# Where the ring splits of a sequence's second half stand, and how many weight-rounding steps follow each product

## The chip, the cores and the metric

The kernel runs on one core of one Trainium2 chip, in one launch. The metric is the device time of that core in microseconds; each run is one execution, and the figure quoted for a kernel is the median of its runs. The profile comes from one further execution.

## What is computed

For 4 sequences of 768 tokens and 384 features, three layers follow each other. Cut to what matters here:

```python
x = delta_rule_attention(q, k, v, beta)          # 8 heads of 48, 768 steps
h = gelu_tanh(x @ w_in)                          # 384 -> 1024
u, v = h[..., :512], h[..., 512:]
v_n = (v - mean(v)) / sqrt(var(v) + 1e-6) * g_ln
v_s = einsum('ts,bsd->btd', w_sg, v_n) + b_sg    # mixing along the 768 tokens
x = x + (u * v_s) @ w_out                        # gates, then the projection
xk, xr = shifted_mix(x, mu_k), shifted_mix(x, mu_r)
out = sigmoid(xr @ w_r) * (relu(xk @ w_k) ** 2 @ w_v)
```

All products are made to float32 precision: each operand is split into a high and a low part (fp32r), and three TensorE products (high by high, high by low, low by high) are summed.

## The kernel before, in words

**Three stages.** The first (to about 340 us of the profile) runs the attention scan together with `x @ w_in`; it writes the normed `v` of each 128-token chunk to DRAM (`vn_d`) and `u` to `u_d`. The second (about 311 to 491 us) is the mixing stage, which the change touches. The third computes the last layer and is not changed.

**The mixing stage.** A sequence `b` has six token chunks `c` and two halves `t` of 384 output tokens each. `mix(b, t, d)` (L1067) makes one mixing product for 128 of the 512 features: 18 matmuls over the six chunks (`mix_mm`, L974), left operand the split chunk (`g` in the profile, "the ring"), right operand the split `w_sg` half (`sw0h`, `sw0l` for t = 0, `ws1h`, `ws1l` for t = 1). Its gates follow: on DVE `w` = product times `g_ln` plus `b_sg` (L1077), times `u` (L1079); on ACT the high part `gh` (L1080); on DVE the low part `gl` (L1083), which is issued one product later. `project(b, t)` (L1091) makes the half's projection: three products of 12 matmuls each (L151), each added into `xT` by DVE (L1099). On TensorE the order per sequence is: `begin`, which makes chunks 0 to 3 of all four products of t = 0 (48 matmuls, L984); the projection of the sequence before, half 1; the rest of the four t = 0 products; the t = 1 products d = 0, 1, 2; the projection of half 0; the t = 1 product d = 3. In the last sequence the projection of half 0 comes behind d = 3.

**The ring.** It has nine slots. A chunk of the next sequence is loaded from `vn_d` into a staging tile `st` by SP (L246) and split by `to_ring` (L907): ACT copies the high part (L120), and the low part is a subtraction, by DVE for chunks 0 and 3, by POOL for the others (L123). Chunks 0 to 2 are split behind `mix(b, 1, 1)` (`VD`), chunks 3 to 5 behind the last gates, those of `mix(b, 1, 3)`. The slots of chunks 3 to 5 are those which the current sequence's chunks 0 to 2 leave, so a split also waits until `mix(b, 1, 3)` has been read from them. "Boundary 0-1" below is the passage from sequence 0 to 1, and so on.

**The rounding jobs.** The weights `w_k`, `w_r` and `w_v` come as pairs of 32-bit words and are rounded beside the mixing stage (`narrow`, L154): a load into `raw`, an ACT copy (L164), four DVE steps (L169, L171, L173, L175), an integer addition by POOL (L177), the high part by ACT (L181), the low part by POOL (L182), a store to DRAM (L203). Blocks are 256 or 384 columns wide. `side(n)` (L1032) issues up to n DVE steps of jobs that are ready, with the other engines' instructions of a job as they come up; it is called behind each mixing product (`SD[0]` = 1) and behind each of the three products of a projection (`SD[1]` = 5). `turns` counts these places; a job's operation that is to be spaced comes one turn later in any case:

```python
            elif isinstance(c, tuple) and c[0]:
                e[0], e[2] = turns[0] + 1, c[1]
```

**What sets the order.** Every engine runs its instructions in the order in which this code issues them; in the mixing stage the order of PE, ACT, DVE, POOL and SP is as written, and no scheduler moves them. The last stage's inputs (`xm_hi`, L120) use memory that the jobs' `raw` buffers give back, so the first of them waits for the last store.

Of the kernel before, what the change touches and what calls it, by code (L numbers as in the profile page):

```python
# [40 lines left out]
EVERY = 12  # L41
NMIX = 12
LATE = 100
PUT = 2
BUDGET = 1.62
SLOT = 5.315
GSTEP = 3
# [14 lines left out]
NRAW = 3  # L62
NNA = 3
PD = 2
SD = (1, 5)
CS = (5, 4)
VF = (0, 3)
VD = 1
# [18 lines left out]
def fused_kernel(  # L87
# [66 lines left out]
    def narrow(dram, i, j, hi, lo, cw=CW, pool=stg, parts=None):  # L154

        w = CW if pool is stg else cw
        raw = pool.tile([P, 2 * w], U32, name="raw", bufs=NRAW)
        nc.sync.dma_start(out=raw[:, :2 * cw], in_=dram[i * P:(i + 1) * P, j:j + cw].bitcast(U32))  # L160
        w_lo = vw(raw, 0, [(2, cw)])
        w_hi = vw(raw, 1, [(2, cw)])
        yield 0
        yield 0, lambda: A.activation(w_lo.bitcast(I32), w_lo, AF.Copy, scale=2.0 ** -29)  # L164
        a = pool.tile([P, w], U32, name="na", bufs=NNA if pool is stg else 2)[:, :cw]
        af = a.bitcast(F32)
        t1 = cw / 1920 + 0.16
        t2 = cw / 960 + 0.16
        V.tensor_scalar(a, w_hi, 0x7FFFFFFF, None, op0=ALU.bitwise_and)  # L169
        yield t1  # L170
        V.tensor_scalar(af, af, E_LO_F, E_HI_F, op0=ALU.max, op1=ALU.min)  # L171
        yield t1
        V.tensor_scalar(a, a, 3, 0x3FFFFFFF, op0=ALU.logical_shift_left, op1=ALU.bitwise_and)  # L173
        yield t1
        V.scalar_tensor_tensor(a, w_hi, 0xC0000000, a, op0=ALU.bitwise_and, op1=ALU.bitwise_or)  # L175
        yield t2
        yield hops[0], lambda: G.tensor_tensor(a.bitcast(I32), a.bitcast(I32), w_lo.bitcast(I32), op=ALU.add)  # L177
        if hi is None:
            hi, lo = (raw[:, e * cw:e * cw + cw].bitcast(F32R) for e in range(2))
            parts.append(raw[:, :2 * cw].bitcast(F32).rearrange("p (x n) -> p x n", x=2))  # L180
        yield 1 + hops[0], lambda: A.activation(hi, af, AF.Copy)  # L181
        yield hops[0], lambda: G.tensor_tensor(lo, af, hi.bitcast(F32), op=ALU.subtract)  # L182

    def resident(dram, pool, name, nblk, n, j0=0, j1=None):
# [9 lines left out]
    def scratch(dram, name, nblk, n, cw=CW, pool=stg):  # L194

        d = dp.tile([nblk, P, 2, n], F32, name=name + "_d")

        def job(i, j):
            parts = []
            yield from narrow(dram, i, j, None, None, cw, pool, parts=parts)  # L200

            def put():
                nc.sync.dma_start(out=d[i, :, :, j:j + cw], in_=parts[0])  # L203

            yield PUT, put

        return d[:, :, 0], d[:, :, 1], [lambda i=i, j=j: job(i, j) for i in range(nblk) for j in range(0, n, cw)]

# [16 lines left out]
    hops = [1]  # L225
# [806 lines left out]
    def side(n):  # L1032

        while n > 0:
# [12 lines left out]
            c = next(e[1], None)  # L1047
            if c is None:
                live.remove(e)
                e[3].append(turns[0] + 1)  # L1050
            elif isinstance(c, tuple) and c[0]:
                e[0], e[2] = turns[0] + 1, c[1]
            elif isinstance(c, tuple):
                c[1]()
            else:
# [11 lines left out]
    def mix(b, t, d):  # L1067
# [3 lines left out]
            pt = ps.tile([P, HF], F32, name="ms")  # L1071
        for c in range(c0, 6):
            mix_mm(pt, b, t, d, c)
        if d == 0:
            gs[b, t] = [mp.tile([P, 4, DM], F32R, name=x) for x in ("gh", "gl")]
        w = vr.tile([P, DM], F32, name="w", bufs=2)
# [8 lines left out]
        if t == 1 and d == 3:  # L1085
            side(1)
            owing.pop()()
        side(SD[0])
        turns[0] += 1

    def project(b, t):  # L1091
        gh, gl = gs.pop((b, t))
        for f in range(3):
# [3 lines left out]
                             for c in range(4)])  # L1097
            xs = xT[:, b, f, 1 + t * DM:1 + t * DM + DM]
            V.tensor_tensor(xs, xs, pt[:, :DM], op=ALU.add)  # L1099
            side(SD[1])  # L1100
            turns[0] += 1

    load_u(0, 0)
# [1 line left out]
    for k, (b, t) in enumerate(halves):  # L1105
# [7 lines left out]
        for d in range(4):  # L1113
# [6 lines left out]
            if t == 1 and b + 1 < B:  # L1120
                if d == VD:
                    for c in range(3):
                        load_v(b + 1, c)
                    for c in range(3, 6):
                        fetch_v(b + 1, c)
                if d == 3:
                    for c in range(3, 6):
                        load_v(b + 1, c)
        while k == 7 and (live or lanes[1][0]):
            side(999)  # L1130
            turns[0] += 1
# [144 lines left out]
```

## Time and profile before

| | us |
|---|---|
| median of 3 runs | 739.75 |
| lowest and highest run | 736.57, 740.77 |
| the profiled execution's own time | 733.87 |
| its span, first to last instruction | 732.2 |
| TensorE busy in it | 679.5 (93%) |
| VectorE busy in it | 504.9 (69%) |

The profiled execution's time is 1.7 us over its span and 5.88 us under the median of the runs. The busy shares are means over all three stages; the mixing stage is read by itself, from the timeline of each engine. Times within the profile are us from the start of the span; a start of one instruction behind another on the same engine tells how late a queue is.

### The profile page before, as it was taken

The page shows a single profiled execution, that of the slowest core. Times are in us where ns is not written, and L with a number is a line of the kernel's source. Part 1 is how long each engine was busy: PE and PEld are TensorE (multiplying, and loading weights), DVE is VectorE, ACT ScalarE, POOL GpSimd, SP SyncE. Part 2 cuts the span into 40 slices and gives each one's busy share as a digit, 9 for nine tenths or more (in the row PEclk, how much of TensorE's full clock was granted, in tenths as well). Part 3 has the DMA queues.
Part 4 walks back from the last instruction along what each step waited for, and adds up shares of the span by engine and source line. Part 5 has one row for each costly group of instructions (what it writes and reads, how often), then busy time and mean ns, then how long its engine had stood idle before and what let it go on. Part 6 is the DMA issues. An engine that isn't in the chain of part 4 may idle for free.

```text
span 732.2 us, 24481 instructions
## 1 busy us (share of the span) xinstructions
PE 679.5 (93%) x10669; PEld 616.3 (84%) x10669; DVE 504.9 (69%) x992; ACT 366.7 (50%) x696; POOL 201.6 (28%) x257
## 2 busy tenths in 40 slices
PE   2567899999989999999999798999999999999998
PEld 2536678888879888899999698998989898999997
DVE  6999999876968965215969697879555564636251
ACT  2237576766757768734323233248354453625140
POOL 3133554443434553231353546340000000000000
PEclk9989999999999999999999999999999999999999
DMA  8503454455565557278645655539000000000000
GB/s 251 105 30 97 130 156 131 116 170 152 161 174 139 162 156 206 63 191 269 244 159 198 220 179 191 188 110 231 33 11 31 14 21 22 23 23 11 33 12 32
DMA packets 80938, 88.71 MB, mean 121 GB/s; under 512 B 24704, under 2 KB 63616, under 8 KB 80832
## 3 DMA queue, kind: packets, MB, share of 16 engines
q1 hardware_dynamic: 75520, 77.33, 35.2%
q0 software_dynamic: 5312, 9.83, 5.2%
q8 instruction: 83, 1.36, 0.8%
q14 instruction: 23, 0.19, 0.1%
HBM read 56.60 MB, written 25.82 MB: 113 GB/s over the span
## 4 chain that ended last, share of the span: by engine, by line
PE 76%; DVE 11%; issue 5%; DMA 4%; POOL 2%; ACT 1%; SPq 0%; POOLq 0%; ACTq 0%; DVEq 0%
PE ms L151 35%; PE ms L705 8%; PE ms L653 7%; PE ms L979 6%; PE ms L581 4%; PE rk L539 3%; PE sps L567 3%; PE rk L552 3%; PE rk L516 2%; PE ms L336 2%; PE ms L474 2%; DVE sg L358 1%; PE qk L519 1%; PE ms L744 1%; DVE w L1077 1%
## 5 line engine op out<-in xcount | busy, mean ns | idle before, releaser
L151 PE MATMUL ms<-wvh,sl 128*128 128x384 f32 x192 | 64.7, 337 | 0.0
L151 PE MATMUL ms<-wvl,sh 128*128 128x384 f32 x192 | 64.6, 337 | 0.0
L151 PE MATMUL ms<-wvh,sh 128*128 128x384 f32 x192 | 64.6, 336 | 0.0
L979 PE MATMUL ms<-sw0h,g 128*128 128x384 f32 x192 | 53.2, 350 | 7.6 <-ACT g L120 6.8
L177 POOL TENSOR_TENSOR na<-na,raw 128x256 int32<-128x256 int32 (+2 forms) x43 | 35.5, 826 | 89.4 <-DVE na L175 35.5
L151 PE MATMUL ms<-xm_hi,sw0h 128*128 128x512 f32 x144 | 56.3, 391 | 0.4 <-ACT xm_hi L120 0.4
L151 PE MATMUL ms<-xm_lo,sw0h 128*128 128x512 f32 x144 | 56.2, 390 | 0.2 <-DVE xm_lo L123 0.2
L151 PE MATMUL ms<-xm_hi,sw0l 128*128 128x512 f32 x144 | 56.1, 390 | 0.0
L123 DVE TENSOR_TENSOR sl<-sg,sh 128x512 fp32r<-128x512 f32 x48 | 33.0, 691 | 25.2 <-ACT sh L120 25.1
L979 PE MATMUL ms<-ws1h,g 128*128 128x384 f32 x192 | 49.9, 335 | 0.0
L1212 DVE TENSOR_TENSOR sg<-sg,ms 128x384 f32<-128x384 f32 x24 | 13.3, 553 | 50.8 <-PE ms L151 50.8
L358 DVE TENSOR_TENSOR sg<-sg,Yt 128x512 f32<-128x512 f32 (+4 forms) x72 | 43.5, 616 | 1.5
L120 ACT ACTIVATE sh<-sg 128x512 fp32r<-128x512 f32 x48 | 30.1, 631 | 28.2 <-DVE sg L1195 28.2
L979 PEld LDWEIGHTS ms<-sw0h,g 128*128 128x128 f32 x192 | 36.5, 197 | 9.1 <-ACT g L120 7.4
L1194 ACT ACTIVATE sg<-ms 128x512 f32<-128x512 f32 x48 | 28.6, 598 | 27.1 <-PE ms L151 24.1
L1080 ACT ACTIVATE gh<-w 128x384 fp32r<-128x384 f32 x32 | 16.8, 525 | 50.0 <-DVE w L1079 50.0
L1195 DVE TENSOR_TENSOR sg<-sg 128x512 f32<-128x512 f32 x48 | 33.1, 693 | 11.0 <-ACT sg L1194 10.8
L336 PEld LDWEIGHTS ms<-kT 64*32 64x32 f32 x640 | 19.5, 129 | 23.9 <-issue 17.0
L532 POOL TENSOR_SCALAR_AFFINE_SELECT SQ<-SQ 64x512 f32<-64x512 f32 x36 | 26.1, 724 | 48.9 <-ACT SQ L531 47.7
L181 ACT ACTIVATE raw<-na 128x256 fp32r<-128x256 f32 (+2 forms) x31 | 13.5, 436 | 51.3 <-POOL na L177 51.2
L345 ACT ACTIVATE sg<-ms 128x256 f32<-128x256 f32 x32 | 17.6, 578 | 41.2 <-PE ms L338 41.1
L338 PE MATMUL ms<-kT 64*32 64x64 f32 (+1 forms) x640 | 22.4, 232 | 16.4 <-issue 16.4
(244 smaller groups left out, 2203.1 us busy)
## 6 DMA issues: line engine op xcount, KB each, us to landing
u_d<-ug SPq DMA_DIRECT2D x24, 256.0 KB, 4.3
u<-u_d SPq DMA_DIRECT2D x16, 384.0 KB, 5.6
vn_d<-v SPq DMA_DIRECT2D x22, 256.0 KB, 2.8
vk<-in_vk_dram SPq DMA_DIRECT2D x24, 192.0 KB, 4.0
vk<-in_vk_dram SPq DMA_DIRECT2D x12, 384.0 KB, 4.8
st<-vn_d SPq DMA_DIRECT2D x18, 256.0 KB, 3.6
out_dram<-sg SPq DMA_DIRECT2D x24, 192.0 KB, 1.9
kT<-in_kt_d_dram SPq DMA_DIRECT2D x8, 512.0 KB, 4.6
```

Of the source, the lines that this page charges most:

```text
L120: A.activation(hi, src, AF.Copy)
L123: eng_lo.tensor_tensor(lo, src, hi.bitcast(F32), op=ALU.subtract)
L151: T.matmul(pt, lhsT=a, rhs=b, start=(i == 0), stop=(i == n - 1))
L177: yield hops[0], lambda: G.tensor_tensor(a.bitcast(I32), a.bitcast(I32), w_lo.bitcast(I32), op=ALU.add)
L336: T.matmul(gps[r:r + 32, p, c0:c1], lhsT=t[r:r + 64, u, 0:32], rhs=t[r:r + 64, u, c0:c1], start=True, stop=True)
L358: V.tensor_tensor(tv, vw(a_t, a_off, a_dims), vw(b_t, b_off, b_dims), op=ALU.mult)
L581: T.matmul(yps[b0:b0 + 64, (0, 1, 2, 6, 3, 4, 5, 7)[p], :], lhsT=cur[h][:, p, 0:64], rhs=cur[h][:, p, D:], start=True, stop=True)
L653: T.matmul(vstat[g, b], lhsT=a[:, c], rhs=w[:, c], start=first, stop=last)
L705: T.matmul(vstat["u"][:, 2 * P * d:2 * P * d + 2 * P], lhsT=w[:, c, ds_], rhs=a[:, c].rearrange("p b t -> p (b t)"), start=first, stop=last)
L979: T.matmul(pt[:, :DM], lhsT=v[:, ds_], rhs=w, start=(c == 0 and i == 0), stop=(c == 5 and i == 2))
L1194: A.activation(r, pt, AF.Relu)
L1195: V.tensor_tensor(r, r, r, op=ALU.mult)
```

## The change

Five edits, all of which act in the mixing stage alone (in the first stage `hops` is 1, and every operation has the spacing that it had):

1. `load_v` for chunks 3 to 5 is called inside `mix(b, 1, 3)`, behind its matmuls and ahead of its gates, and no more behind them.
2. Behind a mixing product `side` may issue 1 step in half 0 and 2 in half 1 (before: 1). Behind each product of a projection it may issue 6 for the projection of a half 1 and 3 for that of a half 0 (before: 5).
3. A job's spaced operations keep the spacing that they ask for. That of the high part is written as 2 turns (it was one turn in effect), that of the store as 1 (as in effect before).
4. A finished job's lane may start its next job in the same turn, not one later.
5. Constants: `SD` and `PUT` go, `SDM` and `SDP` come; `SDH` is used nowhere.

```diff
-PUT = 2
...
-SD = (1, 5)
+SDM = (1, 2)
+SDP = (6, 3)
+SDH = 2
...
-        yield 1 + hops[0], lambda: A.activation(hi, af, AF.Copy)
+        yield 2, lambda: A.activation(hi, af, AF.Copy)
...
-            yield PUT, put
+            yield 1 + hops[0], put
...
-                e[3].append(turns[0] + 1)
+                e[3].append(turns[0])
             elif isinstance(c, tuple) and c[0]:
-                e[0], e[2] = turns[0] + 1, c[1]
+                e[0], e[2] = turns[0] + c[0], c[1]
...
         for c in range(c0, 6):
             mix_mm(pt, b, t, d, c)
+        if t == 1 and d == 3 and b + 1 < B:
+            for c in range(3, 6):
+                load_v(b + 1, c)
...
-        side(SD[0])
+        side(SDM[t])
...
-            side(SD[1])
+            side(SDP[1 - t])
...
-                if d == 3:
-                    for c in range(3, 6):
-                        load_v(b + 1, c)
```

**DVE at boundary 1-2**, from the second addition of the projection of sequence 1, half 0, on. `g_7404` before and `g_7373` in the change are the same tile, chunk 3 of sequence 2. Lines of the changed kernel stand 1 to 4 higher (L1099 is L1103, L1077 is L1081, L1083 is L1087, L123 is L124). Before:

```order
L1099 TENSOR_TENSOR xT<-xT,ms 128x384
L171 TENSOR_SCALAR na<-na 128x384
L173 TENSOR_SCALAR na<-na 128x384
L175 SCALAR_TENSOR_TENSOR na<-raw,na 128x384
L1077 SCALAR_TENSOR_TENSOR w<-ms,g_sb,b_sb 128x384
L1079 TENSOR_TENSOR w<-w,u 128x384
L1083 TENSOR_TENSOR gl<-w,gh 128x384 x2
L123 TENSOR_TENSOR g_7404<-st_7264,g_7404 128x512
```

And in the change:

```order
L1103 TENSOR_TENSOR xT<-xT,ms 128x384
L172 TENSOR_SCALAR na<-na 128x384
L174 TENSOR_SCALAR na<-na 128x384
L176 SCALAR_TENSOR_TENSOR na<-raw,na 128x384
L1103 TENSOR_TENSOR xT<-xT,ms 128x384
L124 TENSOR_TENSOR g_7373<-st_7245,g_7373 128x512
L1081 SCALAR_TENSOR_TENSOR w<-ms,g_sb,b_sb 128x384
L1083 TENSOR_TENSOR w<-w,u 128x384
L1087 TENSOR_TENSOR gl<-w,gh 128x384
L170 TENSOR_SCALAR na<-raw 128x256
L1087 TENSOR_TENSOR gl<-w,gh 128x384
```

The split has passed the two gates and both low parts, and stands directly behind the last addition. Counted over the whole of sequence 1, from the first addition of the projection of sequence 0, half 1, up to the first gate of `mix(1, 1, 3)` before and up to the split in the change, DVE's queue holds 34 rounding steps before and 26 in the change. The same count for sequence 2 is 32 before and 35 in the change.

**ACT at the same place.** In the change:

```order
L165 ACTIVATE raw<-raw 128x384
L182 ACTIVATE raw<-na 128x256 x2
L121 ACTIVATE g_7373<-st_7245 128x512
L121 ACTIVATE g_7376<-st_7247 128x512
L121 ACTIVATE g_7379<-st_7249 128x512
L1084 ACTIVATE gh<-w 128x384
```

The three high parts of the ring stand ahead of the last `gh` and behind two high parts of rounding jobs; before, they stood behind that `gh` and one more high part.

**DVE behind the projection of sequence 1, half 1**, the first of its three products. In the change:

```order
L1103 TENSOR_TENSOR xT<-xT,ms 128x384
L176 SCALAR_TENSOR_TENSOR na<-raw,na 128x256
L170 TENSOR_SCALAR na<-raw 128x384
L172 TENSOR_SCALAR na<-na 128x384
L174 TENSOR_SCALAR na<-na 128x384
L176 SCALAR_TENSOR_TENSOR na<-raw,na 128x384
L170 TENSOR_SCALAR na<-raw 128x384
L1103 TENSOR_TENSOR xT<-xT,ms 128x384
```

Six steps lie between two additions where four lay before. Behind the second addition there are six against four, behind the third five against four. From the first addition to the low part of `mix(2, 0, 3)` it is 20 steps against 16.

## Rows read from the trace of the kernel before

**Rows 1.** The page's first part: busy us (share of span) xinstructions, engines by line.

```profile
PE 679.5 (93%) x10669; PEld 616.3 (84%) x10669; DVE 504.9 (69%) x992; ACT 366.7 (50%) x696; POOL 201.6 (28%) x257
```

**Rows 2.** Waits of PE, 310 to 510 us: waited for, total us, times, longest.

```profile
PE ms L979 <- ACT g L120: 6.8, 2, 4.8
PE ms L979 <- DVE g L123: 0.8, 2, 0.5
```

**Rows 3.** Busy time by stretch: us, PE, PEld, DVE, ACT, POOL, PEclk, DMA, GB/s.

```profile
358.49:369.96 11.47, 11.47 (x67) 11.47 (x67) 7.33 (x15) 4.03 (x9) 5.68 (x6) 1.00 0.73 236
396.23:414.68 18.45, 13.37 (x67) 12.53 (x67) 14.63 (x24) 5.80 (x13) 12.63 (x12) 0.91 0.63 202
440.93:455.45 14.52, 12.02 (x67) 11.38 (x67) 11.80 (x21) 5.21 (x11) 9.94 (x10) 1.00 0.60 208
410.40:414.60 4.20, 3.74 (x12) 3.23 (x13) 1.07 (x1) 1.49 (x4) 3.56 (x3) 0.59 0.98 304
```

**Rows 4.** PE's timeline, boundaries 1-2 and 2-3: start us, us, instruction, [idle before <-releaser].

```profile
405.44 0.34 PE L979 MATMUL ms<-sw0h,g 128*128 128x384 f32 x1
410.57 0.51 PE L979 MATMUL ms<-sw0h,g 128*128 128x384 f32 x1 [4.80 <-ACT g L120]
...
434.57 0.34 PE L151 MATMUL ms<-gh,wo_hi 128*128 128x384 f32 x1
...
450.14 0.34 PE L979 MATMUL ms<-sw0h,g 128*128 128x384 f32 x1
452.49 0.44 PE L979 MATMUL ms<-sw0h,g 128*128 128x384 f32 x1 [2.01 <-ACT g L120]
```

**Rows 5.** DVE's timeline, sequences 1 and 2.

```profile
372.28 0.56 DVE L1099 TENSOR_TENSOR xT<-xT,ms 128x384 f32<-128x384 f32 x1 [5.73 <-PE ms L151]
...
402.33 0.35 DVE L171 TENSOR_SCALAR na<-na 128x384 f32<-128x384 f32 x1
...
404.74 0.73 DVE L171 TENSOR_SCALAR na<-na 128x384 f32<-128x384 f32 x1
...
407.46 0.60 DVE L1077 SCALAR_TENSOR_TENSOR w<-ms,g_sb,b_sb 128x384 f32<-128x384 f32 x1
...
410.55 1.07 DVE L123 TENSOR_TENSOR g<-st,g 128x512 fp32r<-128x512 f32 x1 [0.37 <-ACT g L120]
...
433.31 0.55 DVE L1083 TENSOR_TENSOR gl<-w,gh 128x384 fp32r<-128x384 f32 x1
...
448.17 1.25 DVE L175 SCALAR_TENSOR_TENSOR na<-raw,na 128x384 uint32<-128x384 uint32 x1
449.34 0.60 DVE L1077 SCALAR_TENSOR_TENSOR w<-ms,g_sb,b_sb 128x384 f32<-128x384 f32 x1
...
452.47 1.07 DVE L123 TENSOR_TENSOR g<-st,g 128x512 fp32r<-128x512 f32 x1 [0.38 <-ACT g L120]
```

**Rows 6.** ACT's timeline at boundary 1-2.

```profile
409.07 0.52 ACT L1080 ACTIVATE gh<-w 128x384 fp32r<-128x384 f32 x1 [3.26 <-DVE w L1079]
...
409.91 1.66 ACT L120 ACTIVATE g<-st 128x512 fp32r<-128x512 f32 x3
```

**Rows 7.** DVE busy in 372 to 450 us, lines L169, L171, L173, L175 in turn.

```profile
372.00:450.00 78.00, 7.35 (x16) 0.98 0.55 184
372.00:450.00 78.00, 8.05 (x16) 0.98 0.55 184
372.00:450.00 78.00, 7.84 (x17) 0.98 0.55 184
372.00:450.00 78.00, 9.79 (x17) 0.98 0.55 184
```

**Rows 8.** The chain that ended last, at the end of the stage: start us, us, what.

```profile
488.71 2.30 DMA wv_d<-raw
...
491.12 0.64 ACT xm_hi L120
```

**Rows 9.** Waits of ACT, 310 to 510 us.

```profile
ACT raw L181 <- POOL na L177: 49.3, 15, 9.4
```

## The prediction

> **What bounds the kernel now.** I read the page's busy times first: TensorE is busy for 93% of the span, VectorE for 69% [rows 1]. Those are means over three stages, so the next view is what TensorE waits for in the mixing stage. Two waits carry nearly all of it, both in front of a mixing product's matmul: 6.8 us, two times, until ACT has made a high part of the ring, and 0.8 us, two times, until DVE has made a low part [rows 2]. The timeline of TensorE puts them at two places: in front of chunk 3 of sequence 2, and of sequence 3 [rows 4].
>
> Their price is best read by comparing equal work. The last product of a sequence and `begin` of the next are 66 matmuls at each of the three boundaries. They took 11.47 us at boundary 0-1, 18.45 us at 1-2 and 14.52 us at 2-3 [rows 3]. The first shows no idle TensorE (11.47 us busy of 11.47), so the other two lose 6.98 and 3.05 us, 10.03 us together. Of the 6.98 us, 4.80 us are one wait [rows 4]; part of the rest is the clock: behind that wait the granted clock was 0.59 for 4.20 us, where 0.5 is the 1.2 GHz level and 1.00 the 2.4 GHz level [rows 3]. At 2-3 the idle time was shorter and the clock stayed at 1.00.
>
> Why is the ring late? Not for lack of a transfer or of a slot. ACT began the three high parts at 409.91 us, directly behind the last `gh` at 409.07 us [rows 6], and that `gh` had to wait for DVE's gates, which began at 407.46 us [rows 5]. TensorE had begun the last matmul in front of the wait at 405.44 us [rows 4]. So DVE is some 8 us behind TensorE there, and the ring waits in its queue. At the start of the sequence DVE was not late: at 372.28 us it stood idle for 5.73 us until TensorE gave it the first addition [rows 5]. The lateness grows within each sequence and ends there, at `begin`. That is the resource to follow: DVE's queue from this first addition to the split of chunk 3.
>
> **The change, part by part.**
>
> *The split ahead of the gates.* Two gates, two low parts and ACT's last `gh` no longer lie in front of it. DVE reaches the split where it reached the gates before: at 407.46 us less what the steps change, instead of 410.55 us; at boundary 2-3 at 449.34 us instead of 452.47 us [rows 5]. Everything behind the split moves back by its own 1.07 us or less. The gates' results are next used by the projection of half 1, which comes behind `begin`: hidden at 1-2 by the microseconds that the gates gain there, and about in time at 2-3.
>
> *The steps.* Rounding steps took 7.35, 8.05, 7.84 and 9.79 us for 16, 16, 17 and 17 of them [rows 7]: 33.03 us for 66, 0.50 us each. In sequence 1 the queue holds 26 in front of the split, not 34: 8 x 0.50 = 4.0 us earlier. The split of chunk 3 would begin at 407.46 - 4.0 = 403.5 us and end 1.07 us later, at 404.5 us. TensorE needs the high part one matmul behind 405.44 us, at about 405.6 us, and the low part two further on, at 406.0 us. So the wait goes, with 1.4 us to spare, the clock stays up, and the whole 6.98 us come back. In sequence 2 there are 35 for 32: 3 x 0.50 = 1.5 us later. The split begins at 449.34 + 1.5 = 450.8 us and ends at 451.9 us. By the row at 450.14 us TensorE needs the low part at 450.7 us [rows 4], so about 1.2 us of the 3.05 us stay.
>
> *Bounds of a step.* A 384-wide L171 took 0.35 us alone and 0.73 us beside POOL; the longest step in the rows took 1.25 us [rows 5]. At 0.35 us the 8 steps less are worth 2.8 us and the 3 more cost 1.1 us; at 1.25 us it is 10 us and 3.8 us. At the low price the split of 1-2 ends at 405.7 us, still in time, and 0.8 us of the wait at 2-3 stay; at the high price TensorE waits at 2-3 as long as before. I take the mean, since the steps moved are of all four lines.
>
> *More steps behind the projection of a half 1.* In front of the low part of `mix(2, 0, 3)` there are 20 steps for 16, which makes it 2.0 us later at 0.50 us. It ended at 433.31 + 0.55 = 433.9 us [rows 5], so then at 435.9 us. The projection of half 0 begins at 434.57 us [rows 4] and takes this low part with its 11th matmul, 1.8 us on, at 436.3 us. That is hidden, with 0.4 us to spare; at 1.25 us per step it would be 2.5 us late. A wait here would delay TensorE and so shorten the one at 2-3, and the two aren't added.
>
> *Spacing and lanes.* These change the order, not the number of instructions. The extra turn puts the high part of a job further behind POOL's addition; ACT waited for that addition 15 times, 49.3 us in all [rows 9], beside a TensorE that mostly did not wait. I cost it at nothing: ACT has the time, unless the ring's high parts stand behind such a wait (the third rival). SP's loads of the ring's chunks stay in their places among the stores.
>
> *The end of the stage.* The last store landed 2.30 us behind its issue at 488.71 us, and the last stage's first input followed at 491.12 us [rows 8], while TensorE finished its projections. The steps of the last job stand among the last gates in both orders, one place earlier in the change, so the chain should move with TensorE. I cost it at 0, between -0.4 us (the wait is gone) and +2 us.
>
> **Sum.** 6.98 + 3.05 - 1.2 = 8.8 us. The profiled execution took 733.87 us; less 8.8 us that is 725.1 us. It lies 5.9 us under the median of the runs, 739.75 us, and I carry the same difference over to that: 731.0 us. Runs of one kernel lie up to 3 us from their median, so about 0.5%, 3.7 us, is what a measurement of this kernel can tell from no change.
>
> **Rivals.**
>
> *Sequence 2 gives it back.* If its steps run mostly beside POOL's work, at the long price, boundary 2-3 keeps its 3.05 us and the projection of half 0 begins to wait, say 1 us. The row of 0.35 against 0.73 us speaks for it; the mean of 0.50 us, which already holds such steps, against. Then 6.98 - 1.0 = 6.0 us: 733.8 us. The Trainium skill, GPSIMD Engine Reference, section Specifications, says that GpSimd shares its SBUF interfaces with VectorE and contends with DVE instructions in a 2-port mode or with two SBUF inputs. By that rule, packing six steps behind a product whose POOL work runs beside them is no free move; the trace agrees on the stretching, by the two L171 rows.
>
> *The end does not move.* If the last rounding jobs keep their absolute times, the last store still lands at 491 us and TensorE, 9 us early, waits there. Against it: the steps are bound to the gates in DVE's order. For it: a job is longer by one turn, and stores share the transfer engines with the reload of `w_k`. With 7 of the 8.8 us lost it is 738 us.
>
> *The split stops the queue it was put in front of.* DVE can't pass it. ACT's high part of chunk 3 stands behind two high parts of rounding jobs, which wait for POOL; the longest such wait was 9.4 us [rows 9]. If ACT is held so long at both boundaries, DVE, which has no other work to go to, is held with it, the gates come later still, and TensorE waits for the ring some 9 us at each instead of 5.1 and 2.5 us: 10 us more, 750 us. It decides from the point where ACT reaches the split later than about 412 us. Against it: POOL's addition for these two jobs follows DVE steps that stand a projection product ahead of the split, about 3 us before. The Trainium skill, TensorE: Matmul & The Clock Gate, section on the array's architectural detail, states that the queues of ACT and DVE are strictly first in, first out; the trace agrees (high parts at 409.91 us only behind the `gh` at 409.07 us), and it is what makes this rival possible.
>
> *It does not act.* The budgets are upper limits; where no job is ready nothing is issued, and the order shows 0 steps behind one product of each kind. But the split's new place and the 26 for 34 are in the order, so this only trims the sum.
>
> **How the numbers follow.** Forecast 0.60 (both waits mostly gone, 729 to 734 us); sequence 2 gives it back 0.20 (733 to 736 us); the end does not move 0.11 (736 to 741 us); the split stops the queue 0.09 (745 us and more). Faster by over 0.5% is under 736.0 us: the first case, nearly all of the second, a little of the third: 0.79. Within 0.5%: 0.13. Slower: 0.08. The range reaches from 727.5 us (all of 10.0 us, and 2 us of scatter) to 737.5 us (the second case, and part of the third).
>
> **What would show it.** TensorE's 66 matmuls at boundary 1-2 take about 11.5 us with a clock of 1.00, and at 2-3 between 11.5 and 13 us. DVE's split of chunk 3 begins some 2 us ahead of TensorE's need at 1-2 and about with it at 2-3. No wait for `gl` at the projection of sequence 2. The first `xm_hi` comes about 9 us earlier. I am wrong if the span of the mixing stage shrinks and the time doesn't, if DVE stands idle in front of L124 for microseconds, or if a new wait of PE for `gl` is as long as the one removed.

## The result and the profile after

The changed kernel is slower: its median is 742.41 us against 736.41 us for the kernel before (17 runs each), a ratio of 1.0086 with a 95% interval of 1.0062 to 1.0111, or some 6 us. The forecast was 731.0 us, its range 727.5 to 737.5 us. (The ratios here and below are estimated from the single runs; the quotient of two medians differs from them by up to 0.2% and is 1.0081 here.) Its profiled execution has a span of 740.2 us, 8.0 us over the 732.2 us of before.

The 8.0 us are first put in their places. TensorE reached the mixing stage 2.8 us later (314.56 instead of 311.74 us). That is no effect of the change: the program of the first stage is the same, and over the profiles of all kernels of this study with that first stage the same moment lies anywhere from 309.23 to 317.25 us. The rest arose in the mixing stage. The first view is TensorE's waits from there on (what waited, for what: us in total, times, longest), after the change:

```profile
PE ms L980 <- ACT g L121: 5.4, 1, 5.4
PE ms L980 <- DVE g L124: 3.6, 1, 3.6
...
PE ms L152 <- DVE gl L1087: 0.7, 1, 0.7
```

These are the two kinds of wait of [rows 2], each one time instead of two, and in total longer: 9.0 us instead of 7.6. The busy times by stretch say where (columns as in [rows 3]); the stretches are boundary 1-2, the projection of half 0 in sequence 2, boundary 2-3, and two pieces of the last:

```profile
399.02:410.49 11.47, 11.47 (x67) 11.47 (x67) 9.45 (x15) 3.82 (x9) 8.61 (x8) 1.00 0.51 168
430.40:437.74 7.34, 6.62 (x38) 6.30 (x37) 5.24 (x13) 2.28 (x5) 0.74 (x1) 1.00 0.47 161
437.74:462.55 24.81, 15.78 (x68) 14.91 (x67) 15.89 (x25) 7.13 (x16) 11.13 (x10) 0.77 0.47 159
446.40:451.80 5.40, 5.33 (x18) 5.11 (x19) 5.28 (x8) 2.33 (x6) 3.57 (x3) 0.54 0.71 257
459.00:464.50 5.50, 5.32 (x17) 5.32 (x18) 3.87 (x7) 2.17 (x5) 3.64 (x4) 0.50 0.14 49
```

Boundary 1-2 is what the prediction said, to the hundredth: 11.47 us instead of 18.45, no idle TensorE, clock 1.00. But boundary 2-3 takes 24.81 us, 10.3 us more than the 14.52 us of before. Of its 13.34 us over 11.47, 9.03 us are idle time (24.81 less 15.78 us busy), and the other 4.31 us are matmuls at a lower clock: behind the two waits, of 5.45 and 3.58 us, the granted clock was 0.54 and 0.50, at or near the 1.2 GHz level. The projection in front of it is 0.98 us longer, the one behind it 1.09 us (clock again). So: 2.8 - 7.0 + 1.0 + 10.3 + 1.1 - 0.2 (the end of the stage) = 8.0 us.

The question is boundary 2-3. DVE's timeline there:

```profile
433.44 0.61 DVE L1081 SCALAR_TENSOR_TENSOR w<-ms,g_sb,b_sb 128x384 f32<-128x384 f32 x1
...
435.03 0.42 DVE L176 SCALAR_TENSOR_TENSOR na<-raw,na 128x256 uint32<-128x256 uint32 x1
437.35 0.30 DVE L170 TENSOR_SCALAR na<-raw 128x256 uint32<-128x256 uint32 x1 [1.91 <-DMA raw<-in_w_k_dram]
446.45 0.69 DVE L124 TENSOR_TENSOR g<-st,g 128x512 fp32r<-128x512 f32 x1 [8.80 <-ACT g L121]
447.06 0.61 DVE L1081 SCALAR_TENSOR_TENSOR w<-ms,g_sb,b_sb 128x384 f32<-128x384 f32 x1
```

From the gates of one product to those of the next DVE takes 13.6 us, of which it stands idle 1.91 us in front of a job's first step, whose raw words are not there, and 8.80 us in front of a split. This is not the split that the change moved: it is that of chunk 0, behind the product t = 1, d = 1, whose place the change leaves alone. The chain of waits (start us, us, what; pieces of under 0.1 us left out) says what was late:

```profile
434.94 3.05 DMA wk_d<-raw
438.04 0.33 SPq L161
438.42 3.55 DMA wv_d<-raw
442.02 0.33 SPq L161
442.40 3.37 DMA st<-vn_d
445.79 0.64 ACT g L121
```

And SP's timeline shows how the row of the chain began:

```profile
426.77 0.33 SPq L161 DMA_DIRECT2D raw<-in_w_k_dram  x1
427.14 0.43 SPq L204 DMA_DIRECT2D wv_d<-raw  x1
430.67 0.33 SPq L161 DMA_DIRECT2D raw<-in_w_v_dram  x1
431.10 0.56 SPq L204 DMA_DIRECT2D wk_d<-raw  x1
434.56 0.33 SPq L161 DMA_DIRECT2D raw<-in_w_k_dram  x1
...
442.02 0.33 SPq L161 DMA_DIRECT2D raw<-in_w_v_dram  x1
442.40 1.37 SPq L247 DMA_DIRECT2D st<-vn_d  x3
```

A store, then the load of the next job, which goes into a `raw` buffer that a store gives back, so that SP stands until that store has landed; then the next store. The five loads of raw words from 426.77 to 442.02 us follow each other at 3.5 to 4.0 us, each behind a store, and the loads of the ring's chunks 0 to 2 (L247) behind them: 442.40 us instead of 430.14 us before. The waits of SP from 426 to 442.3 us are 14.6 us of 16.3:

```profile
SPq L161 <- DMA wk_d<-raw: 8.4, 3, 3.0
SPq L161 <- DMA wv_d<-raw: 6.2, 2, 3.1
```

In the kernel before SP did the same, only less often. There the ring's loads stood behind these (SP's timeline of before):

```profile
421.06 0.33 SPq L160 DMA_DIRECT2D raw<-in_w_v_dram  x1
421.43 0.56 SPq L203 DMA_DIRECT2D wk_d<-raw  x1
424.92 0.33 SPq L160 DMA_DIRECT2D raw<-in_w_k_dram  x1
427.26 0.56 SPq L203 DMA_DIRECT2D wk_d<-raw  x1
429.76 0.33 SPq L160 DMA_DIRECT2D raw<-in_w_k_dram  x1
430.14 1.37 SPq L246 DMA_DIRECT2D st<-vn_d  x3
```

How much less often can be counted on SP's timeline, from the last of the ring's loads for sequence 2 to the first of those for sequence 3. Before, 8 loads of raw words and 8 stores stand there, and the loads waited 19.7 us for stores in a stretch of 40.2 us. In the change there are 11 and 11, and the loads waited 31.6 us in 53.5 us. So the longer waits for stores are 11.9 of the 13.3 us by which the stretch grew. The times 430.14 and 442.40 us differ by 12.3 us, of which 2.8 us are the later start of the stage: counted from TensorE's first matmul of the stage, the ring's loads go out 9.4 us later.

### The profile page after: what moved, and what is told of

It reads as the page before. It is cut to its first block, busy times and chain, and to the rows that moved or that the text cites. A ratio compares the mean times of both kernels' runs of the same rounds, so it can differ in the third digit from the quotient of the medians.

```text
span 740.2 us, 24476 instructions
## 1 busy us (share of the span) xinstructions
PE 685.4 (93%) x10669; PEld 621.4 (84%) x10669; DVE 507.6 (69%) x992; ACT 366.9 (50%) x696; POOL 204.2 (28%) x257
## 4 chain that ended last, share of the span: by engine, by line
PE 80%; DVE 10%; issue 4%; DMA 3%; POOL 1%; ACT 1%; SPq 0%; POOLq 0%; DVEq 0%; ACTq 0%
PE ms L152 36%; PE ms L980 9%; PE ms L706 8%; PE ms L654 7%; PE ms L582 4%; PE sps L568 3%; PE rk L540 3%; PE rk L553 3%; PE rk L517 2%; PE ms L337 2%; PE ms L475 2%; DVE sg L359 1%; PE qk L520 1%; PE ms L745 1%; DVE w L1083 1%
## 5 line engine op out<-in xcount | busy, mean ns | idle before, releaser
L178 POOL TENSOR_TENSOR na<-na,raw 128x256 int32<-128x256 int32 (+2 forms) x43 | 37.4, 870 | 78.7 <-DVE na L176 36.3
L124 DVE TENSOR_TENSOR sl<-sg,sh 128x512 fp32r<-128x512 f32 x48 | 33.1, 690 | 26.6 <-ACT sh L121 26.5
L1213 DVE TENSOR_TENSOR sg<-sg,ms 128x384 f32<-128x384 f32 x24 | 13.3, 552 | 49.6 <-PE ms L152 49.6
L980 PEld LDWEIGHTS ms<-sw0h,g 128*128 128x128 f32 x192 | 38.1, 206 | 10.0 <-ACT g L121 5.8
L337 PEld LDWEIGHTS ms<-kT 64*32 64x32 f32 x640 | 19.0, 127 | 23.4 <-issue 16.3
L706 PE MATMUL ms<-xl,wiu_hi 128*128 128x256 f32 x144 | 36.9, 296 | 0.0
```

The source lines that it names most:

```text
L124: eng_lo.tensor_tensor(lo, src, hi.bitcast(F32), op=ALU.subtract)
L337: T.matmul(gps[r:r + 32, p, c0:c1], lhsT=t[r:r + 64, u, 0:32], rhs=t[r:r + 64, u, c0:c1], start=True, stop=True)
L706: T.matmul(vstat["u"][:, 2 * P * d:2 * P * d + 2 * P], lhsT=w[:, c, ds_], rhs=a[:, c].rearrange("p b t -> p (b t)"), start=first, stop=last)
L980: T.matmul(pt[:, :DM], lhsT=v[:, ds_], rhs=w, start=(c == 0 and i == 0), stop=(c == 5 and i == 2))
```

## The experiments

Since the median of the kernel before moved between the sets of runs (735.5 to 739.2 us; the second set ran on another chip), the ratios to it in the same set are what is compared. Sets: e1 to e4, e5 to e8, e9 to e12. "Ring's loads" are those of chunks 0 to 2 for sequence 3, in us of the profile. Since TensorE begins the stage anywhere from 309.23 to 317.25 us, "in the stage" counts them from its first matmul there, and this column is the one to compare. "Loads ahead" are the loads of raw words on SP between the ring's loads for sequence 2 and those for sequence 3, for the kernels that issue the ring's loads at the old place on SP. The boundaries are the 66 matmuls, from the first matmul to that of the projection behind them, us. Four parts: S the split ahead of the gates, B the budgets, H the extra turn ("hop") ahead of the high part, L the lane's restart in the same turn.

| kernel | parts | ratio (95%) | ring's loads | in the stage | loads ahead | 1-2 | 2-3 |
|---|---|---|---|---|---|---|---|
| before | none | 1 | 430.1 | 118.4 | 8 | 18.45 | 14.52 |
| the change | S B H L | 1.0086 (1.0062 to 1.0111) | 442.4 | 127.8 | 11 | 11.47 | 24.81 |
| e5 | S | 0.9916 (0.9886 to 0.9946) | 423.0 | 113.8 | 8 | 13.83 | 11.47 |
| e11 | B | 1.0092 (1.0055 to 1.0128) | 441.3 | 124.5 | 11 | 11.47 | 26.14 |
| e12 | L | 1.0121 (1.0087 to 1.0154) | 433.2 | 118.3 | 8 | 19.28 | 17.85 |
| e6 | S B | 0.9993 (0.9964 to 1.0021) | 433.8 | 122.8 | 11 | 11.47 | 19.29 |
| e2 | S B H | 0.9931 (0.9902 to 0.9959) | 429.8 | 112.5 | 7 | 11.47 | 11.45 |
| e3 | S H L | 1.0020 (0.9995 to 1.0044) | 439.1 | 122.7 | 8 | 11.86 | 14.89 |
| e10 | S B L | 1.0088 (1.0054 to 1.0122) | 443.5 | 126.5 | 8 | 19.01 | 20.05 |
| e7 | B H L | 1.0198 (1.0156 to 1.0240) | 438.4 | 128.5 | 11 | 12.04 | 32.12 |
| e4 | S B H L, ring fetched early | 0.9986 (0.9964 to 1.0007) | 424.3 | 108.1 | - | 11.47 | 16.89 |
| e8 | S B H L, ring loaded by ACT | 1.0017 (0.9984 to 1.0050) | 426.6 | 115.3 | - | 11.47 | 19.01 |
| e9 | S B, ring fetched early | 0.9903 (0.9878 to 0.9928) | 422.7 | 108.5 | - | 11.47 | 13.86 |

The theory (A) is that SP's queue holds the ring's loads and the jobs' loads; the rivals are that the moved split holds DVE (B), and that the six steps make DVE late in sequence 2 (C).

### e1, e5: the split alone

Against before; the last hunk is e1's alone, and it acts in the first stage too.

```diff
@@ mix
+        if t == 1 and d == 3 and b + 1 < B:
+            for c in range(3, 6):
+                load_v(b + 1, c)
@@ behind mix
-                if d == 3:
-                    for c in range(3, 6):
-                        load_v(b + 1, c)
@@ narrow
-        yield 1 + hops[0], lambda: A.activation(hi, af, AF.Copy)
+        yield 1, lambda: A.activation(hi, af, AF.Copy)
```

> The kernel before with one edit: the splits of chunks 3 to 5 stand in front of the sequence's last gates; step budgets, spacing and lanes are those of before. Theory A (SP's queue is what went wrong): the loads of the ring's chunks 0 to 2 for sequence 3 are issued at about 430 us as before, because the order on SP is that of before; the split alone gains. The 66 matmuls of boundary 1-2 take 14 to 16 us (before 18.45 us), since DVE is two gates earlier but still has 34 steps ahead of the split; those of 2-3 take 11.5 to 12 us (before 14.52 us). Time 729 to 732 us. Theory B (the split in front of the gates holds DVE at ACT's high part, and that is the loss): boundary 2-3 takes over 20 us here too, time 738 us or more.

> The split in front of the last gates, alone. The kernel of e1_split_alone differed from before in a second place: in the first stage, too, a job's high part came one turn earlier, because the line of the spacing was written as 1 there and not as 1 plus the hop of that stage. Here the first stage is that of before. Theory A (the gain is the split's, at the boundaries): 66 matmuls at 1-2 take 13.5 to 14.5 us, at 2-3 11.5 to 12 us, and the time is 728 to 732 us. Theory D (much of that gain was the first stage's edit): the mixing stage starts 1.5 us or more later than in e1 and the time is 733 us or more.

Measured: e1 729.29 us, ratio 0.9876 (0.9836 to 0.9915), boundaries 13.81 and 11.66 us; e5 728.75 us, 0.9916. Both as theory A had it (e1's first boundary is just under its 14 to 16 us), and rival B is out: in front of the moved split DVE did not stand idle in either kernel. The two boundaries of e5:

```profile
392.13:405.96 13.83, 12.03 (x67) 11.40 (x67) 13.55 (x23) 5.12 (x12) 10.20 (x10) 1.00 0.53 169
433.10:444.57 11.47, 11.47 (x68) 11.47 (x67) 11.16 (x20) 4.84 (x11) 8.38 (x8) 1.00 0.58 195
```

Boundary 2-3 has lost all of its 3.05 us, 1-2 4.62 of its 6.98 us; there TensorE still waits 0.6 us for a high and 1.2 us for a low part. Theory D had given 733 us or more for e5, and is out at that size; whether e1's edit of the first stage brought anything is open: the intervals overlap, and the boundaries are alike.

### e2: the lanes undone

Against the change:

```diff
-                e[3].append(turns[0])
+                e[3].append(turns[0] + 1)
```

> The changed kernel with one part undone: a lane's next job starts one turn behind the end of the last, as before, so that its load of raw words no longer stands directly behind the store whose buffer it takes. Theory A (SP's queue): three such loads instead of six stand between boundary 1-2 and the loads of the ring's chunks, at 3.9 us each; those are issued at 430 to 433 us instead of 442.4 us, boundary 2-3 takes 12 to 15 us instead of 24.8 us, and the time is 730 to 734 us. Theory C (six steps behind each product of a projection make DVE and POOL late in sequence 2): the steps stay, so boundary 2-3 stays over 20 us and the time at 740 us or more.

Measured: 733.6 us, ratio 0.9931. The ring's loads go out at 429.76 us, behind 7 loads of raw words instead of 11, and both boundaries are free of idle time:

```profile
400.15:411.62 11.47, 11.47 (x68) 11.47 (x67) 11.05 (x17) 3.71 (x9) 9.02 (x9) 1.00 0.62 197
437.92:449.37 11.45, 11.45 (x67) 11.45 (x67) 11.28 (x18) 5.33 (x13) 9.28 (x9) 1.00 0.61 203
```

One line of the program is the difference between 24.81 and 11.45 us. What the line did is not quite what was expected of it: the loads still wait for stores. SP's waits from 418 to 430 us, ahead of the ring's loads:

```profile
SPq L161 <- DMA wk_d<-raw: 7.3, 2, 4.1
SPq L161 <- DMA wr_d<-raw: 3.0, 1, 3.0
```

Over the whole stretch between the ring's loads for sequences 2 and 3 they are 19.3 us for 7 loads, 2.8 us each, against 2.9 us each in the change; fewer of them stand ahead of the ring. Against rival C this kernel says only a part: the budgets of six steps are in place, but with jobs that start later DVE's queue holds 32 steps in sequence 2 up to the split of chunk 3, as before, not the 35 of the change. e9 below is the better test. What A did not foresee is the end: a projection at the end of the stage waits 2.10 us for a `gl`, and the last stage 3.02 us for `xm_hi`:

```profile
482.93 0.44 PE L152 MATMUL ms<-gl,wo_hi 128*128 128x384 f32 x1 [2.10 <-DVE gl L1087]
490.80 0.49 PE L152 MATMUL ms<-xm_hi,sw0h 128*128 128x512 f32 x1 [3.02 <-ACT xm_hi L121]
```

The first `xm_hi` begins at 490.12 us (491.12 before, [rows 8]), but this profile's stage begins 5.5 us later than that of before (317.25 instead of 311.74 us). Counted from there, the first `xm_hi` comes 6.5 us earlier, and TensorE is through with its mixing products 11.45 us earlier, so it waits. From the end of these products (472.54 us) to the end of the span it is 260.3 us, 6.5 us more than in before. This is the rival "the end does not move", by half, in a kernel that had the gain to lose.

### e3: the budgets undone

Against the change:

```diff
-SDM = (1, 2)
-SDP = (6, 3)
+SDM = (1, 1)
+SDP = (5, 5)
```

> The changed kernel with one part undone: 1 step behind each mixing product and 5 behind each product of a projection, as before; split, spacing and lanes stay those of the change. Theory A (SP's queue): four loads of raw words stand in front of the ring's, not six; these are issued at 433 to 436 us, boundary 2-3 takes 14 to 18 us; boundary 1-2 has its 34 steps back in front of the split and takes 13 to 16 us. Time 735 to 739 us. Theory C (the budgets are the loss): boundary 2-3 comes down to 11.5 to 13 us and the time to 732 us or less.

Measured: 741.45 us, ratio 1.0020, so 0.7% better than the change. The time is over A's 735 to 739 us. Boundary 2-3 is in A's range (14.89 us), and 1-2 is better than it (11.86 us, not 13 to 16; 30 steps stood in front of the split, not 34). The ring's loads come at 439.09 us, later than said (122.7 us into the stage, 4.3 us later than before), and the loss has moved: DVE stood 3.83 us in front of a job's first step (L170, for raw words) and 3.01 us in front of the split; the projection ahead of the boundary took 10.76 us, and the last stage waited 6.0 us for `xm_hi`. The first of these waits is for a load of SP's row; what made the end late was not followed further.

### e4, e8: the ring's loads taken out of the row

Against the change, e4 first, then e8 (in `fetch_v`):

```diff
-VF = (0, 3)
+VF = (0, 0)
```

```diff
-        vsts[b, c] = staged(vn_d[b, c], HF)
+        vsts[b, c] = turn(sts, [P, HF])[:, 0:HF]
+        nc.scalar.dma_start(out=vsts[b, c], in_=vn_d[b, c])
```

> The changed kernel with one more edit: the loads of the ring's chunks 0 to 2 for the next sequence are issued in front of the sequence's product t = 0, d = 0 instead of d = 3, so that on SP one load of raw words stands ahead of them behind boundary 1-2, not six. Budgets, spacing, lanes and the split stay those of the change. Theory A (SP's queue): the loads are issued at about 423 us and are in long before ACT asks; DVE does not stand in front of the split; boundary 2-3 takes 11.5 to 13.5 us, that of 1-2 stays at 11.47 us, and the time is 729 to 733 us. Theories B and C (DVE held by the moved split, or late through its steps): boundary 2-3 stays over 20 us, the time at 740 us or more.

> The changed kernel with the ring's loads for the next sequence issued by ACT and not by SP, at the same place in the program: they no longer stand behind SP's loads of raw words. All else is the change. Theory A: chunks 0 to 2 for sequence 3 are issued by 432 us instead of 442.4 us; DVE is not held in front of their split; boundary 2-3 takes 11.5 to 15 us instead of 24.8 us; time 731 to 736 us. The upper end is there because ACT itself now waits for the staging tiles of chunks 3 to 5, some 3 to 4 us, with a gate's high part behind it. Theories B and C: boundary 2-3 stays over 20 us, the time at 740 us or more.

Measured: 736.67 us, ratio 0.9986, and 736.65 us, 1.0017. The loads went out at 424.25 and 426.59 us as expected, and DVE's 8.80 us in front of the split are 0.7 us in both. Boundary 2-3 falls to 16.89 and 19.01 us, not to the 11.5 to 13.5 and 11.5 to 15 us that A gave, and the times are over A's ranges (729 to 733 and 731 to 736 us). DVE's timeline of e8 shows what A had left out:

```profile
437.38 0.30 DVE L170 TENSOR_SCALAR na<-raw 128x256 uint32<-128x256 uint32 x1 [4.26 <-DMA raw<-in_w_k_dram]
438.38 0.69 DVE L124 TENSOR_TENSOR g<-st,g 128x512 fp32r<-128x512 f32 x1 [0.71 <-ACT g L121]
```

The row of pairs on SP still delays the jobs' own loads. Where the ring no longer waits for them, DVE stands in front of a rounding step (L170) for 4.26 us, and the split stands behind that step. In e4 the same step waits 3.51 us. So theory A was too narrow: SP's row of pairs is later than DVE's order of steps presumes, and whichever load DVE meets first carries the wait. What the rest of boundary 2-3 consists of was not undone part by part: in e8 TensorE waits 4.09 us there for the low part of chunk 3, in e4 3.80 us for a high part.

### e6, e9: split and budgets, without spacing and lanes

Against the change; the last two lines are e9's alone.

```diff
-        yield 2, lambda: A.activation(hi, af, AF.Copy)
+        yield 1 + hops[0], lambda: A.activation(hi, af, AF.Copy)
...
-                e[3].append(turns[0])
+                e[3].append(turns[0] + 1)
...
-VF = (0, 3)
+VF = (0, 0)
```

> The split in front of the last gates and the new step budgets, with the spacing and the lanes of before: the changed kernel without two parts that the prediction costed at nothing. Theory A (spacing and lanes filled SP's queue): on SP the loads of raw words come in twos behind two stores, so fewer of them wait for a store issued just before; the ring's loads are issued by 434 us of the profile; boundary 1-2 takes 11.5 us, 2-3 11.5 to 13 us, and the time is 729 to 733 us, what the prediction said for the whole change. Theory C (the six steps are the loss): boundary 2-3 takes over 15 us and the time is 737 us or more. The last stage may begin later than in before, since jobs restart a turn later: up to 3 us of this time.

> The kernel of e6_split_budgets (split in front of the gates, new budgets, spacing and lanes of before) with one more edit: the ring's loads of chunks 0 to 2 are issued in front of the product t = 0, d = 0 instead of d = 3. In e6 they were issued at 433.75 us behind loads of raw words that waited for stores, and DVE stood 5.86 us in front of the split. Theory A (SP's queue is what the budgets overfill): they are issued by 425 us; DVE stands less than 1 us in front of the split of chunk 0; boundary 2-3 takes 11.5 to 14 us instead of 19.29 us; time 727 to 731 us. Theory C (the six steps themselves make DVE late in sequence 2): boundary 2-3 stays over 17 us and the time at 733 us or more.

Measured: e6 734.42 us, ratio 0.9993: the budgets, which in the prediction were worth 4 us at 1-2, give back all that the split alone brings (0.9916). Boundary 1-2 does get its 11.47 us, but 2-3 takes 19.29, in C's range, not in A's, and the time lies between the two. DVE's timelines tell the two apart; e6 first, then e9:

```profile
437.88 0.69 DVE L124 TENSOR_TENSOR g<-st,g 128x512 fp32r<-128x512 f32 x1 [5.86 <-ACT g L121]
```

```profile
435.47 0.29 DVE L170 TENSOR_SCALAR na<-raw 128x256 uint32<-128x256 uint32 x1 [1.11 <-DMA raw<-in_w_k_dram]
436.45 0.69 DVE L124 TENSOR_TENSOR g<-st,g 128x512 fp32r<-128x512 f32 x1 [0.69 <-ACT g L121]
```

In e9 the same steps stand in the same order on DVE (34 in sequence 2 up to the split of chunk 3, in both), and only three loads on SP are ahead of their old place. The wait of 5.86 us goes, boundary 2-3 takes 13.86 us, the ratio is 0.9903 (731.56 us), just over the 727 to 731 us expected. So most of the budgets' cost is SP's too, and rival C is out at the size of the loss; what is left for it in e9 is at most the 2.39 us that boundary 2-3 takes over 11.47 us.

### e7: the split undone

Against the change:

```diff
@@ mix
-        if t == 1 and d == 3 and b + 1 < B:
-            for c in range(3, 6):
-                load_v(b + 1, c)
@@ behind mix
+                if d == 3:
+                    for c in range(3, 6):
+                        load_v(b + 1, c)
```

> The changed kernel with the split of chunks 3 to 5 put back behind the last gates; budgets, spacing and lanes stay those of the change, and with them SP's order. Theory A: the ring's loads for sequence 3 stand behind six loads of raw words and are issued at 440 to 446 us as in the change; boundary 2-3 takes 20 to 27 us; boundary 1-2 takes 12 to 15 us; time 742 to 747 us. Theory B (it is the moved split that holds DVE): boundary 2-3 takes 15 us or less and the time is 737 us or less.

Measured: 749.39 us, ratio 1.0198, worse than either theory's time; the loads came at 438.38 us, and DVE stood 8.65 us in front of the same split. Boundary 2-3 takes 32.12 us:

```profile
433.41:465.53 32.12, 15.88 (x67) 14.50 (x67) 15.32 (x27) 7.96 (x17) 12.34 (x12) 0.69 0.45 151
```

The moved split saves 1.1% in the change, where it saves 0.84% alone; the intervals don't tell the two apart.

### e10: the spacing undone

Against the change:

```diff
-        yield 2, lambda: A.activation(hi, af, AF.Copy)
+        yield 1 + hops[0], lambda: A.activation(hi, af, AF.Copy)
```

> The changed kernel with one part undone: a high part comes one turn behind POOL's addition in the mixing stage, as before; split, budgets and lanes stay those of the change. Theory A (SP's queue): five loads of raw words instead of six stand in front of the ring's loads for sequence 3, each behind a store issued just before; these are issued at 435 to 440 us, boundary 2-3 takes 15 to 22 us, and the time is 736 to 742 us. Theory F (it is the extra turn that makes stores and loads late): the ring's loads are issued by 432 us, boundary 2-3 takes 13 us or less, and the time is 733 us or less.

Measured: 745.6 us, ratio 1.0088, the same as the change's 1.0086. Theory F is out: in the change the extra turn costs nothing that can be measured. The loss lies otherwise, though: the ring's loads for sequence 2 are late as well (398.58 us instead of 387.94 us in the change, of which 2.5 us are the later start of the stage), DVE stands in front of a split in sequence 1 too (5.54 us, and 4.93 us in sequence 2), and boundary 1-2 takes 19.01 us. Theory A had the right place and too small a size.

### e11, e12: budgets alone, lanes alone

Against before, e11 first, then e12:

```diff
-SD = (1, 5)
+SDM = (1, 2)
+SDP = (6, 3)
...
-        side(SD[0])
+        side(SDM[t])
...
-            side(SD[1])
+            side(SDP[1 - t])
```

```diff
-                e[3].append(turns[0] + 1)
+                e[3].append(turns[0])
```

> The kernel before with the new budgets alone; the split stays behind the last gates, spacing and lanes are those of before. The prediction's own price of a step: the gates at 1-2 begin 4 us earlier, so boundary 1-2 takes 13 to 15 us (before 18.45 us). Theory A (SP's queue): the ring's loads for sequence 3 come behind more loads of raw words, at 432 to 436 us; DVE stands 4 to 7 us in front of their split; boundary 2-3 takes 20 to 26 us (before 14.52 us); time 738 to 744 us. The prediction's view (SP's loads keep their places): boundary 2-3 takes 14.5 to 16 us and the time is 731 to 734 us.

> The kernel before with one edit: a lane's next job starts in the turn in which the last one ends. Theory A: with 5 and 1 steps as budgets the jobs leave SP time to catch up: two loads of raw words stand in front of the ring's loads for sequence 3, which are issued by 431 us; the boundaries take 14 to 20 us (1-2) and 11.5 to 15 us (2-3); time 732 to 738 us, within 0.5% of before. Theory G (starting the next job in the same turn is harmful by itself, because its load stands directly behind the store whose buffer it takes): DVE stands over 4 us in front of a job's first step, and the time is 740 us or more.

Measured: e11 744.98 us, ratio 1.0092; e12 747.46 us, ratio 1.0121. The budgets alone clear boundary 1-2 wholly, more than expected. Boundary 0-1 takes 14.00 us instead of 11.47, where DVE had stood 2.27 us in front of a job's first step. They lose more at 2-3, where DVE stood 6.34 us in front of the split; the ring's loads came at 441.26 us, later than said (6.1 us later in the stage than before):

```profile
402.19:413.66 11.47, 11.47 (x68) 11.47 (x67) 8.22 (x19) 4.67 (x10) 6.09 (x7) 1.00 0.67 208
440.96:467.10 26.14, 14.46 (x68) 12.99 (x68) 17.38 (x26) 7.79 (x16) 13.52 (x12) 0.77 0.53 175
```

e12 is a miss for theory A, which had said "within 0.5% of before": two loads of raw words do stand in front of the ring's, at 433.19 us instead of the 431 us expected. Counted in the stage that is no later than before (118.3 against 118.4 us), so here the ring's loads are not the loss. Theory G had the time right (740 us or more), and the place nearly: DVE stood 3.03 us (not over 4) in front of a job's first step.

```profile
431.61 0.29 DVE L170 TENSOR_SCALAR na<-raw 128x256 uint32<-128x256 uint32 x1 [3.03 <-DMA raw<-in_w_k_dram]
```

Boundary 2-3 is 3.3 us longer than before, 1-2 0.8 us. The largest part lies at the end: from the stage's last mixing matmul to the end of the span it is 259.0 us, 5.3 us more than in before, with a wait of 3.6 us for `xm_hi` in it. Why the last jobs end later there was not followed further.

## Why the prediction was wrong, step by step

- **The split ahead of the gates: right.** Alone it is worth 0.84% (e5). The third rival feared that DVE would stand in front of the split of chunk 3; it did not, in any kernel (0.12 us at most). The prediction's sign of being wrong, DVE idle in front of L124, did come, at another split and for another reason.
- **The steps in sequence 1: right.** Fewer steps in front of the split clear boundary 1-2. In the change the split of chunk 3 began at 405.61 us and ended at 406.94 us, ahead of TensorE's need at 408.8 us (399.02 us plus the 9.8 us that [rows 4] gives): 1.9 us to spare, where 1.4 was said. The price also held: 0.48 us each after the change (26.0 us for 54 steps in the same 78 us), against 0.50.

```profile
405.61 1.33 DVE L124 TENSOR_TENSOR g<-st,g 128x512 fp32r<-128x512 f32 x1
```

- **The step that failed** is "SP's loads of the ring's chunks stay in their places among the stores", with "I cost it at nothing". Their place in the row of turns did stay; what stands in front of them did not. The prediction counted what the budgets move on DVE and not what they move on SP, where each job is a load and a store: 11 pairs instead of 8 stand ahead of the ring in the change, and in e6, e7 and e11, which have the new budgets too (7 and 8 in e2 and e10, whose jobs stand otherwise; why the count differs there was not followed). The lanes issue the next load closer behind a store: with them a load of that stretch waited 2.9 to 3.3 us for one on average (the change, e3, e7, e10, e12), without them 2.3 to 2.8 us (before, e1, e2, e5, e6, e11). The ring's loads went out 12.3 us later (9.4 us in the stage), DVE stood 8.80 us, and boundary 2-3 lost 10.3 us. Undoing the lanes alone takes that back (e2), and so does, for the budgets' part, issuing the ring's loads ahead of the row (e9).
- **More steps in sequence 2: not refuted, but small beside the loss.** 1.2 us of the 3.05 us were to stay at 2-3 for three more steps of 0.50 us. An estimate from the trace of the change agrees: its split of chunk 3 ended at 459.13 us, and without the 10.71 us that DVE stood idle would have ended at 448.4 us, 0.9 us behind TensorE's need at 437.74 plus 9.8 us. In e9, with 34 steps, 2.39 us stay; in e2, where none stays, there are 32, as before. What e6 spends beyond, it spends through SP.
- **The `gl` of `mix(2, 0, 3)`: a near miss.** It was to be in time by 0.4 us; TensorE waited 0.72 us.
- **The level.** The median of 739.75 us that the sum started from was that of three runs; over 17 runs it is 736.41 us. That is 3.3 us, and not why the sum failed.
- **The end of the stage** did not bite in the change, since TensorE was late itself: 0.23 us of waiting against 0.67 us before. It bit in e2, where TensorE was early.

So of the four parts, the split is a gain of its own, the budgets and the lanes cost more than they bring (0.9% and 1.2% alone), and the extra turn was not run alone. In the change, taking the lanes back gains 1.5%, taking the budgets back 0.7%, taking the split back loses 1.1%. The parts do not add: 0.9916 times 1.0092 is 1.0007 and e6 has 0.9993, but the extra turn, worth nothing beside the lanes of the change (e10), gains 0.6% beside those of before (e2 against e6).

The trace of before held the answer, in a view that I did not read: SP's own waits from 355 to 470 us.

```profile
SPq L160 <- DMA wk_d<-raw: 24.3, 9, 4.5
SPq L203 <- POOL raw L182: 23.8, 10, 9.1
SPq L160 <- DMA wv_d<-raw: 14.7, 5, 5.1
```

44 us of 115 went into loads behind a store (24.3, 14.7 and 5.2 us for `wr_d`, in a row not shown), and 23.8 us more into stores that waited for POOL. That was the place to ask what more pairs would cost.

The Trainium skill, DMA: Bandwidth & Descriptors, section "Anatomy of one DMA — SWDGE (gpsimd) path", states that transfer engines don't wait on semaphores: any such wait is made by the issuing sequencer, ahead of the dispatch. The trace agrees for SP: the load at 438.04 us went out as the store issued at 434.94 us had landed 3.05 us later, and the ring's loads, which needed neither, stood behind it. The Trainium skill, TensorE: Matmul & The Clock Gate, section on the array's architectural detail, gives ACT's and DVE's queues as strictly first in, first out; the 8.80 us, with gates behind that needed nothing of the split, agree.

Four kernels beat both: e1, e5, e9 and e2; the intervals of e5 overlap with those of each of the others. With one edit, the split in front of the gates alone, e5 is 0.84% faster than before and 1.7% faster than the change by their ratios.

## What to carry to other kernels

Where an edit changes how often or how early background work starts, count what it puts on the queue that issues transfers, in the order in which it stands there: a load that reuses a buffer whose store stands just in front of it holds that queue until the store has landed (3.0 to 3.6 us in the rows shown), and every later transfer with it. Issue the loads on which the bound engine depends ahead of the row (e9), or let fewer pairs stand in front of them (e2). When profiles are compared, count times from the start of the stage: here it moved by up to 8 us with nothing changed ahead of it. And a bundle is worth undoing part by part: here no kernel with more parts was measurably faster than the one with a single part.

## What the runs showed that was not expected

- Freeing the ring's loads moved the wait, it did not end it: 8.80 us at the split became 0.7 us there and 4.26 us at a job's first step (e8). DVE takes its work in order, and its idle time showed the earliest late input only.
- Idle time costs more than its length: at 2-3, 9.03 us of idle TensorE cost 13.34 us, as the granted clock was 0.54 and 0.50 in the 5.40 and 5.50 us behind the two waits; the projection behind took 1.09 us more besides. After the wait of 0.72 us at 433.05 us the clock of that stretch stayed at 1.00.
- The lanes, a change of one turn for the start of a load, which was costed at nothing, move the time as much as the parts that were meant to move DVE's work: 1.2% alone, beside 0.84% for the split and 0.9% for the budgets.
